# One load for Wq, held transposes, two QK bursts and twelve output buffers in a gated attention and token-MLP kernel

## Chip, cores and metric

The kernel runs on one core of one Trainium2 chip. The metric is device time in microseconds (us). Before: 175.59 us, the median of four executions. Most executions of this kernel lie within 0.3 us of their median.

The words used below: PE is the tensor engine, DVE the vector engine, ACT the scalar engine, SP the engine that issues the DMAs. A DMA lands when its semaphore reports it complete. An evacuation is the copy of a PE result out of its accumulator (`ps`) by DVE or ACT. bn_stats is the DVE instruction that collects the layer norm's mean and variance. A QK burst is a run of tiled matmuls that sums the logits, an AV burst one that sums the weighted values. The gelu bubble is the wait of PE for the last gelu (on ACT) between the two MLP products. A combine is the last line of the reference for one row tile. The granted clock is the share of PE's full clock that the trace shows; here it is 1 or a half. An execution counts as slow when it is over 1.5% above the fastest of the same kernel; slow ones are left out of the ratios, but not out of the medians.

## The reference, cut to what matters

```python
# x: (2048, 512) bf16; H = 32 heads of 16; window of 8 keys, dilation 2
g = sigmoid((x * gate_w).sum(-1))                  # one gate per row
a = attention(x @ wqkv) @ wo                       # 8 logits per query and head
b = transpose(gelu(layernorm(x)^T @ w1 + b1) @ w2 + b2)   # MLP over the 2048 rows, F = 1792
out = g * a + (1 - g) * b
```

On PE this is 48 groups of projections (four groups are split in two), two MLP matrix products of 224 matmuls each, 16 groups for wo, and small sums. The logits and the weighted values are products on DVE, which PE then sums with 0/1 matrices in tiled mode, several small matmuls side by side.

## The kernel before

A small scheduler written in Python orders the operations of every engine when the kernel is built; the order is static. The parts that the change touches:

```python
ld_x("sp", 0, 2); ld_x("sp", 2, 2)      # rows 0..511, 256 KB each
ld_w("sp", 0, 0, 2)                     # Wq, first half of the contraction, 256 KB
l_wq = ld_w("sp", 0, 2, 2)              # Wq, second half
l_wk = ld_w("sp", 1, 0, 4)              # Wk, 512 KB
ld_xt(1); ld_x("sp", 4, 4)              # DMA transposes of x and plain x blocks
ld_xt(2); ld_x("sp", 8, 4)
ld_xt(3); ld_x("sp", 12, 4)
ld_w("sp", 2, 0, 4)
# ... 7 warm-up matmuls, PE transposes of rows 0..511, evacuations on DVE and ACT ...
# first Q matmuls: halves of the contraction, so the first 16 need only the first half of Wq
for (dts, tps) in [((0, 1), (0,)), ((0, 1), (1,)), ((2, 3), (0, 1))]: ...
# ... QK: after every two DVE products (4.4 us each) one PE burst of 32 tiled matmuls; 4 bursts.
# The gate: 16 tiled matmuls on their own. ...
ds_out = [sch.dsem("out%d" % k) for k in range(4)]   # 4 output buffers, one semaphore each
for h in range(2): ...                  # the last tile goes out in two pieces of 256 columns
for d in ds_out: e.wait_ge(d.handle, 16 * n_)        # SP, at the very end
```

## Time and profile before

| read from | value |
|---|---|
| time, median of 4 | 175.59 us |
| span of the profile | 174.28 us |
| first Q matmul starts | 6.67 us |
| last output matmul starts | 171.09 us |
| last store lands | 173.81 us |

The first thing to settle is what bounds the kernel. The page of the kernel before says it in its busy shares (part 1) and in the chain that ended last (part 4):

```profile
PE 167.1 (96%) x1003; PEld 78.9 (45%) x1022; DVE 144.9 (83%) x146; ACT 74.3 (43%) x101; POOL 0.9 (0%) x8
...
PE 91%; DMA 3%; ACT 2%; issue 1%; SPq 1%; DVE 0%; DVEq 0%
```

DVE is 83% busy, but it takes none of the chain. The waits of PE, longest first, of the kernel before:

```profile
PE ps L610 <- DMA arena<-in_A_wqkv_dram: 1.5, 1, 1.5
PE ps L524 <- POOL arena L424: 1.1, 1, 1.1
PE ps L837 <- issue: 0.5, 3, 0.2
PE ps L876 <- ACT arena L850: 0.2, 1, 0.2
```

The columns are total us, number of waits, longest wait. Two waits at the front make 2.6 us of 3.3; L610 is the first Q matmul, and Wq is what it waits for. The timeline of PE at the front, kernel before (start, us, what, and in brackets the idle time ahead and what ended it):

```profile
1.06 3.07 PE L524 MATMUL ps<-arena 128*128 128x512 bf16 x7 [1.06 <-POOL arena L424]
3.96 1.17 PE L536 MATMUL ps<-arena 128*128 128x128 bf16 x16
6.67 3.66 PE L610 MATMUL ps<-arena 128*128 128x256 bf16 x32 [1.53 <-DMA arena<-in_A_wqkv_dram]
10.38 1.89 PE L587 MATMUL ps<-arena 128*128 128x512 bf16 x8
```

The four QK bursts are the lines of L688 in the PE timeline further on, x32 each, between ordinary matmuls:

```profile
43.05 1.91 PE L688 MATMUL ps<-arena 128*32 128x512 bf16 x32
44.89 7.10 PE L587 MATMUL ps<-arena 128*128 128x512 bf16 x31
51.91 1.91 PE L688 MATMUL ps<-arena 128*32 128x512 bf16 x32
53.98 6.85 PE L837 MATMUL ps<-arena 128*128 128x512 bf16 x31 [0.16 <-issue]
60.77 1.91 PE L688 MATMUL ps<-arena 128*32 128x512 bf16 x32
62.84 6.85 PE L837 MATMUL ps<-arena 128*128 128x512 bf16 x31 [0.16 <-issue]
69.62 1.91 PE L688 MATMUL ps<-arena 128*32 128x512 bf16 x32
```

No burst waits for its products: DVE does not set PE's pace here.

### The profile page before, as it was taken

What the parts mean: (1) busy time and instruction counts of PE and PEld (TensorE: products, weight loads), DVE (VectorE), ACT (ScalarE), POOL (GpSimd) and SP (SyncE); (2) the same over time, 40 slices, a digit from 0 to 9 for tenths busy, and PEclk for the clock granted to TensorE, in tenths of its full rate; (3) what the DMA queues carried; (4) which work ended last, traced back from release to release, by engine and by line L of the source; (5) the groups of instructions that cost most, each with busy time, mean ns of one, the idle gap of its engine ahead of it and who ended that gap; (6) DMA issues with size and microseconds to landing.
All of it is one profiled execution on the core that took longest, in us unless ns stands there. A gap on an engine that the chain in (4) does not pass through costs nothing.

```text
span 174.3 us, 2443 instructions
## 1 busy us (share of the span) xinstructions
PE 167.1 (96%) x1003; PEld 78.9 (45%) x1022; DVE 144.9 (83%) x146; ACT 74.3 (43%) x101; POOL 0.9 (0%) x8
## 2 busy tenths in 40 slices
PE   7699999999999999999999999999999999999993
PEld 3565554454444444444444443444444444444441
DVE  1707789799999999378999999999999999638824
ACT  2276668578367211679311315133521622270010
POOL 1000000000000000000000000000000000000000
PEclk9999999999999999999999999999999999999999
DMA  5999999920007079999999000073474370004413
GB/s 157 233 252 240 286 308 271 274 36 6 0 0 211 4 221 183 164 253 181 283 290 290 17 4 0 0 208 104 113 211 113 101 211 0 0 0 154 150 60 120
DMA packets 44862, 24.87 MB, mean 143 GB/s; under 512 B 7860, under 2 KB 44852, under 8 KB 44852
## 3 DMA queue, kind: packets, MB, share of 16 engines
q1 hardware_dynamic: 44852, 24.72, 58.9%
q8 instruction: 8, 0.13, 0.3%
q14 instruction: 2, 0.02, 0.0%
HBM read 18.88 MB, written 2.10 MB: 120 GB/s over the span
## 4 chain that ended last, share of the span: by engine, by line
PE 91%; DMA 3%; ACT 2%; issue 1%; SPq 1%; DVE 0%; DVEq 0%
PE ps L876 28%; PE ps L837 28%; PE ps L587 21%; PE ps L893 7%; PE ps L688 4%; DMA arena<-in_A_wqkv_dram 3%; PE ps L610 2%; PE ps L784 1%; ACT L653 1%; ACT arena L598 1%; PE ps L642 1%; SPq L437 1%; ACT arena L850 0%; DVE arena L917 0%; DVEq L331 0%
## 5 line engine op out<-in xcount | busy, mean ns | idle before, releaser
L876 PE MATMUL ps<-arena 128*128 128x512 bf16 x217 | 48.8, 379 | 0.6 <-ACT arena L850 0.2
L837 PE MATMUL ps<-arena 128*128 128x512 bf16 x218 | 48.0, 379 | 0.6 <-issue 0.5
L587 PE MATMUL ps<-arena 128*128 128x512 bf16 x171 | 38.5, 380 | 0.4
L776 DVE TENSOR_TENSOR arena<-arena 128x8192 bf16<-128x8192 bf16 x8 | 35.0, 4417 | 0.0
L681 DVE TENSOR_TENSOR arena<-arena 128x8192 bf16<-128x8192 bf16 x8 | 34.8, 4420 | 0.0
L876 PEld LDWEIGHTS ps<-arena 128*128 128x128 bf16 x224 | 21.5, 98 | 27.4 <-issue 1.2
L837 PEld LDWEIGHTS ps<-arena 128*128 128x128 bf16 x224 | 21.7, 98 | 27.0 <-issue 1.3
L940 ACT ACTIVATE arena<-ps,arena 128x512 bf16<-128x512 f32 x16 | 12.4, 776 | 37.5 <-PE ps L876 37.5
L587 PEld LDWEIGHTS ps<-arena 128*128 128x128 bf16 x176 | 19.5, 114 | 18.6 <-ACT arena L595 0.7
L598 ACT ACTIVATE arena<-ps 128x512 bf16<-128x512 f32 x32 | 18.9, 596 | 10.2 <-PE ps L587 10.1
L850 ACT ACTIVATE arena<-ps,arena 128x512 bf16<-128x512 f32 x14 | 9.6, 687 | 30.7 <-PE ps L837 30.6
L926 DVE SCALAR_TENSOR_TENSOR arena<-ps,arena 128x512 bf16<-128x512 f32 x15 | 11.2, 750 | 9.0 <-PE ps L893 7.5
L561 DVE BATCH_NORM_STATS2 arena<-arena 128x6 f32<-128x512 bf16 x16 | 10.1, 681 | 10.3 <-DMA arena<-in_A_x_dram 10.3
L893 PE MATMUL ps<-arena 128*128 128x512 bf16 x59 | 13.2, 379 | 0.1
L824 ACT ACTIVATE arena<-ps 128x512 bf16<-128x512 f32 (+1 forms) x7 | 8.0, 1146 | 4.3 <-PE ps L784 4.2
L803 DVE TENSOR_TENSOR arena<-arena 128x2048 bf16<-128x2048 bf16 x8 | 9.7, 1216 | 0.0
L806 DVE TENSOR_TENSOR arena<-arena 128x2048 bf16<-128x2048 bf16 x8 | 9.7, 1215 | 0.0
L729 DVE TENSOR_TENSOR arena<-arena 128x256 bf16<-128x256 bf16 (+4 forms) x16 | 7.8, 506 | 2.0 <-ACT arena L743 1.7
L810 DVE TENSOR_TENSOR arena<-arena 128x2048 bf16<-128x2048 bf16 x8 | 9.4, 1216 | 0.0
L893 PEld LDWEIGHTS ps<-arena 128*128 128x128 bf16 x60 | 5.9, 98 | 7.1
L595 ACT ACTIVATE arena<-ps 128x512 bf16<-128x512 f32 x12 | 7.1, 596 | 2.7 <-PE ps L587 2.7
L688 PE MATMUL ps<-arena 128*32 128x512 bf16 x128 | 7.6, 380 | 0.0
(56 smaller groups left out, 64.6 us busy)
## 6 DMA issues: line engine op xcount, KB each, us to landing
arena<-in_B_w_dram SPq DMA_DIRECT2D x7, 1024.0 KB, 9.7
arena<-in_B_w_dram SPq DMA_DIRECT2D x8, 896.0 KB, 5.1
arena<-arena SPq DMA_DIRECT2D x16, 131.5 KB, 5.9
out_dram<-arena SPq DMA_DIRECT2D x15, 128.0 KB, 1.7
arena<-in_A_x_dram SPq DMA_DIRECT2D x3, 512.0 KB, 4.6
arena<-in_A_wqkv_dram SPq DMA_DIRECT2D x2, 512.0 KB, 5.9
arena<-in_A_x_dram SPq DMA_DIRECT2D x2, 256.0 KB, 3.1
arena<-in_A_wqkv_dram SPq DMA_DIRECT2D x2, 256.0 KB, 4.8
```

Of the source, the lines that this page charges most:

```text
L561: A("dve", (lambda t_: (lambda e: e.bn_stats(out=ST6[:, t_, :], in_=X[:, t_, :])))(t), 0.7, reads=["x%d" % t], writes=["st6_%d" % t], name ...
L587: ins = e.matmul(ps[:, bank, :], lhsT=lhsT, rhs=XT[:, sb, dt, :], start=(dt == 0), stop=(dt == 3))
L598: return lambda e: e.activation(out=dst, in_=ps[:, bank, :], func=AF.Copy)
L681: return lambda e: e.tensor_tensor(out=PBL[buf], in0=in0, in1=in1, op=ALU.mult)
L688: ins = e.matmul(ps[32 * c:32 * c + 32, 4 + wl, :], lhsT=RP, rhs=PBL[buf][:, wl, c * 512:(c + 1) * 512], start=(dl == 0), stop=(dl == 3), ...
L776: return lambda e: e.tensor_tensor(out=PV[buf], in0=in0, in1=in1, op=ALU.mult)
L803: A("dve", (lambda b_: (lambda e: e.tensor_tensor(out=PV[b_][:, 0, :, :], in0=PV[b_][:, 0, :, :], in1=PV[b_][:, 1, :, :], op=ALU.add)))(bu ...
L837: ins = e.matmul(ps[:, bank, :], lhsT=W1W[:, slot, st, 128 * e_:128 * e_ + 128], rhs=X[:, st, :], start=(st == 0), stop=(st == NST - 1))
L876: ins = e.matmul(ps[:, bank, :], lhsT=W2S[slot][:, ft, 128 * e_:128 * e_ + 128], rhs=UT[:, ft, :], start=(ft == 0), stop=(ft == NFT - 1))
L893: ins = e.matmul(ps[:, WB(i), :], lhsT=OT[:, t, 128 * i:128 * i + 128], rhs=WO[:, t, :], start=(t == 0), stop=(t == 3))
L926: A("dve", (lambda i_: (lambda e: e.scalar_tensor_tensor(out=OUTS[:, i_ % 4, :], in0=ps[:, WB(i_), :], scalar=col(G, i_), in1=T1[:, i_, :] ...
L940: A("act", (lambda i_, bank_: (lambda e: e.activation(out=T1[:, i_, :], in_=ps[:, bank_, :], func=AF.Identity, scale=col(OMG, i_), bias=co ...
```

## The change

The intent: get Wq in sooner with one load that transposes do not disturb, free the front evacuations from bn_stats, pay for fewer switches into tiled mode, and never let an output buffer hold up a combine. Its core (cuts marked):

```diff
-        ld_w("sp", 0, 0, 2)
-        l_wq = ld_w("sp", 0, 2, 2)
-        l_wk = ld_w("sp", 1, 0, 4)
-        ld_xt(1)
-        ld_x("sp", 4, 4)
+        l_wq = ld_w("sp", 0, 0, 4)
+        ld_w("sp", 1, 0, 4)
+        ld_x("sp", 4, 4)
+        ld_xt(1, deps=[l_wq])
   ... (x blocks now ahead of the transposes; gate, bias and wo loads chained in order)
-        last_main[0] = front
-        for (dts, tps) in [((0, 1), (0,)), ((0, 1), (1,)), ((2, 3), (0, 1))]:
+        last_main[0] = A("pe", f_warm_on(NWARM2, 0), ...)          # NWARM2 = 3
+        for tp_ in range(2):
+            order0 = [(dt, tp_, dl) for dl in range(4) for dt in range(4)]
   ... (bn_stats of the first four tiles only after the evacuations on DVE)
   ... (the 16 normalisations get a low priority, to fill DVE while burst 1 runs)
+            def f_qk4(e, wh=wh):                                    # 64 matmuls, two bursts in all
+                r = [f_qkr(wh, dl, QKB[wh][dl])(e) for dl in range(4)]
+                return r + [f_gz(e)] if wh == 0 else r              # the gate behind the first
-        ds_out = [sch.dsem("out%d" % k) for k in range(4)]
+        ds_out = [sch.dsem("out%d" % k) for k in range(NOUT)]       # NOUT = 12
-            for h in range(2):
-                cs = slice(256 * h, 256 * h + 256)
+            for h, cs in enumerate((slice(0, 256), slice(256, 384), slice(384, 512))):
```

The products of a whole burst now need four buffers at once, so two more were laid over memory that is free at that time, and the output buffers were laid over the attention weights.

## The prediction

> **What bounds it now.** The tensor engine: the chain of waits is PE for 91%, and the PE timeline is continuous from 6.67 us (first Q matmul) to 171.36 (last output matmul), 164.7 of 174.3 us. The list of waits gives PE 3.3 us of idling, 2.6 of it before 6.67. DVE is 83% busy but costs PE no wait at the bursts. Only three places can pay: the front, extra cost inside the PE stream, and the tail (2.9 us).
>
> **Front: -0.75 us.** The first Q matmul waits 1.5 us for Wq (list of waits). The DMA issues show landings x 3.79 and 4.46, Wq halves 6.53 and 7.20, Wk 9.08. Undisturbed packets move 350 to 380 GB/s (0.7 us per 256 KB); from about 4.2 us, soon after the first transpose is issued (3.35), the same 1 KB packets take 66 to 71 ns instead of 47. With transposes held, 512 KB of Wq after 4.46 should land at about 5.9. Front evacuations ahead of bn_stats (680 ns each) are ready by then. The three extra warm-up matmuls end about 5.8. First Q matmul: 5.9.
>
> **Held transposes: +0.15 us (expectation).** The first starts at about 5.9 instead of 3.35, should land at 11.3 to 12.6, and is needed at 5.9 + 3.66 + 3.46 = 13.0. The last, now behind the last x block, should land at 20.6 to 22 (before: 20.88), needed at about 21.7: a stall of 0 to 1 us is possible.
>
> **Bursts: -0.55 us.** Tiled matmuls run 4 abreast, 57 ns each, so their own work stays. In the PE start times, entering a tiled group costs 308 ns against 216 between plain matmuls, leaving it 312: about 0.19 us per group. The Trainium skill ("TensorEngine Tiling (Array Packing)", Key Properties) says that changing the tiling mode drains the engine; the trace agrees, 0.19 us a round trip. Five groups (4 QK, 1 gate) become two: three round trips fewer. DVE cannot refill products while burst 1 runs (4.7 us), but 16 normalisations (0.33 us each) move into that gap. Attention should end about 1.5 us earlier, off PE's path.
>
> **AV bursts: +0.2 us (expectation).** The first AV burst (0.65 us at 106.1) now fills, by luck, the gelu bubble before the second MLP matmul. If it moves out, the bubble shows as a 0.9 us wait.
>
> **Tail: +0.3 us.** Twelve output buffers remove a 0.38 us DVE wait that PE did not feel. The last tile is stored in three pieces instead of two; an issue takes 0.46 us on the DMA queue, already back to back at the end (171.30, 171.69, 172.15), so one more delays the end by 0.3 to 0.45, less a slightly shorter last combine.
>
> **Sum.** 175.7 - 0.75 - 0.55 + 0.15 + 0.2 + 0.3 = 175.0; shaded to 174.8, since the order is made by a static scheduler that gets to fit the moved pieces. Range 173.8 to 176.2. Faster by over 2%: 2%; within 2%: 94%; slower by over 2%: 4%.
>
> **What would show it.** First Q matmul at 5.7 to 6.1, packets at 47 ns until then; no PE wait on x loads between 10 and 25 us; two QK groups of 64, 16 gate matmuls behind the first, no PE wait at either; PE stream first Q to last output matmul 164.1 to 164.5; gelu waits of PE under 0.9 us; tail 3.2 us.
>
> **What would make it wrong.** A burst placed before DVE has its products (PE stalls up to some us, since order is static); a late transpose or Wk; attention so late that DVE paces the last output matmuls.

## The result

The change takes 176.72 us against 175.59 before (medians of four), 1.13 us more. The ratio is 1.0064, with a 95% interval of 1.0047 to 1.0082. Ratios here and below are the mean time of one kernel's fast runs over that of the other's of the same rounds, so not quite the ratio of the medians. That is inside 2%, but outside the range that I gave (173.8 to 176.2), and on the other side of zero.

The page of the kernel after, the same two lines:

```profile
PE 167.9 (96%) x1011; PEld 80.8 (46%) x1029; DVE 145.8 (83%) x147; ACT 77.0 (44%) x103; POOL 0.9 (0%) x8
...
PE 76%; DVE 13%; ACT 6%; issue 3%; DVEq 0%; POOL 0%; POOLq 0%
```

DVE and ACT are in the chain now. That looks like a new bottleneck, but the waits of PE in the kernel after show what it costs:

```profile
PE ps L519 <- POOL arena L427: 1.1, 1, 1.1
PE ps L607 <- DVE arena L557: 0.6, 1, 0.6
PE ps L778 <- DVE arena L804: 0.2, 1, 0.2
PE ps L584 <- issue: 0.2, 1, 0.2
PE ps L831 <- issue: 0.2, 1, 0.2
```

The chain goes through DVE because the first AV burst (L778) waits 0.2 us for it. A chain shows where the last link was, not how tight it was. One releaser here is also a misreading: the first Q matmul (L607) is put down to bn_stats on DVE, an operation whose result it does not read. The landing times show that Wq came in at 6.89, 0.13 us ahead of that matmul, the same distance as before (6.53 to 6.67). The PE timeline of the front, kernel after:

```profile
1.06 3.17 PE L519 MATMUL ps<-arena 128*128 128x512 bf16 x7 [1.06 <-POOL arena L427]
4.02 1.80 PE L531 MATMUL ps<-arena 128*128 128x128 bf16 x16
5.66 0.81 PE L519 MATMUL ps<-arena 128*128 128x512 bf16 x3
7.02 3.66 PE L607 MATMUL ps<-arena 128*128 128x256 bf16 x32 [0.55 <-DVE arena L557]
```

The two bursts, PE timeline of the kernel after. No burst waits for its products here either; the burst matmuls are all there, in two groups:

```profile
44.87 3.64 PE L666 MATMUL ps<-arena 128*32 128x512 bf16 x64
48.33 1.04 PE L636 MATMUL ps<-arena 128*32 128x512 bf16 x16
49.54 4.26 PE L584 MATMUL ps<-arena 128*128 128x512 bf16 x19 [0.17 <-issue]
53.64 15.70 PE L831 MATMUL ps<-arena 128*128 128x512 bf16 x71
69.27 3.64 PE L666 MATMUL ps<-arena 128*32 128x512 bf16 x64
```

A kernel that is one unbroken PE stream can be cut at four milestones, and the pieces add up to the span. These times are from the records of the two traces:

| piece | before, us | after, us | difference | predicted |
|---|---|---|---|---|
| start to first Q matmul | 6.67 | 7.02 | +0.36 | -0.75 |
| first Q to last output matmul (starts) | 164.42 | 163.78 | -0.64 | -0.20 |
| last output matmul (start) to last landing | 2.73 | 3.13 | +0.40 | +0.30 |
| last landing to end of span | 0.47 | 1.04 | +0.57 | 0 |
| span | 174.28 | 174.97 | +0.69 | |

(The -0.20 is -0.55 for the bursts with the two expectations of +0.15 and +0.2.) The middle came out better than I said; the front and the last row came out worse. The table explains 0.69 of 1.13 us. The rest is the front of this one execution of before: the run that was profiled took 176.0 us, 0.4 above the median, and a second profile of the same kernel (run b_same below) had its first Q matmul at 6.12 and a span of 173.79, 1.18 below the kernel after. The granted clock was 0.998 to 1.0 in all four timed executions of the kernel after, so the half clock that comes up below is no part of the 1.13 us.

### The profile page after: what moved, and what is told of

Its sections match the earlier page's. It is cut to its first block, busy times and chain, and to the rows that moved or that the text cites. A ratio compares the mean times of both kernels' runs of the same rounds, so it can differ in the third digit from the quotient of the medians.

```text
span 175.0 us, 2471 instructions
## 1 busy us (share of the span) xinstructions
PE 167.9 (96%) x1011; PEld 80.8 (46%) x1029; DVE 145.8 (83%) x147; ACT 77.0 (44%) x103; POOL 0.9 (0%) x8
## 4 chain that ended last, share of the span: by engine, by line
PE 76%; DVE 13%; ACT 6%; issue 3%; DVEq 0%; POOL 0%; POOLq 0%
PE ps L870 28%; PE ps L584 20%; PE ps L831 9%; PE ps L887 7%; DVE arena L770 5%; PE ps L666 4%; ACT arena L737 2%; PE ps L607 2%; PE ps L519 2%; PE ps L778 1%; DVE arena L723 1%; DVE arena L804 1%; DVE arena L797 1%; DVE arena L800 1%; DVE arena L748 1%
## 5 line engine op out<-in xcount | busy, mean ns | idle before, releaser
L708 ACT ACTIVATE arena<-ps 128x1024 bf16<-128x1024 f32 x4 | 4.0, 1021 | 8.5 <-PE ps L666 4.6
```

## The experiments

All kernels gave correct results. In the first four and in the kernel after, the traces show the same order of PE's groups, of DVE and of ACT apart from the named edit. From f_oldfront on, the order of every engine behind the front is frozen to that of the changed kernel, by giving the scheduler a list, because it otherwise moves bursts and output matmuls at the far end when a load at the front changes. Times are medians of five or six executions.

### 1. The changed kernel with Wq in two loads: a_split

```diff
-        l_wq = ld_w("sp", 0, 0, 4)
+        ld_w("sp", 0, 0, 2)
+        l_wq = ld_w("sp", 0, 2, 2)
   (and the order of the first Q matmuls by halves, as before)
```

> The changed kernel with Wq in two 256 KB loads again and the first Q matmuls in the order of before (first half of the contraction first); the transposes stay held, all else as changed. Theory A (one 512 KB load makes PE wait for the last byte of all of Wq, and without the transposes the first half could land at 5.3 to 5.9 us): first Q matmul at 5.9 to 6.4 us instead of 7.02, then limited by the extra warm-up, and the time falls 0.6 to 1.1 us, to about 175.8. Rival B (Wq itself moves slowly whatever its cut; the cut is innocent): first half lands at 6.5 or later, first Q at 6.7 or later, time within 0.3 us of the changed kernel.

Measured: 176.42 us, ratio to before 1.0039 (1.0017 to 1.0060). The first half landed at 6.03, but the first Q matmul started at 6.88. The clock of PE was at half until 6.74 us in that execution, and the three extra warm-up matmuls, which run ahead of it in program order, started at 5.72, ran mostly at that half clock and held it up. The ratio is 0.0025 below that of the changed kernel (about 0.4 us), with overlapping intervals. Neither theory was cleanly met: the half came early, as A said, and something else held PE.

### 2. The changed kernel without the hold: a_nohold

```diff
-        ld_xt(1, deps=[l_wq])
+        ld_xt(1)
```

> The changed kernel with the first transpose no longer held for Wq: only its wait on Wq is taken out, so it is issued right behind the x block, at about 3.4 us. If transposes in flight slow Wq, as I predicted: Wq lands later than 6.89, at 7.2 to 7.6, and the time rises 0.3 to 0.7 us. If the hold is useless: Wq lands at 6.9 within 0.15 us and the time is the same within 0.15 us, with the transposed x blocks landing 1 to 3 us earlier.

Measured: 176.84 us, ratio 1.0080 (1.0055 to 1.0104). Wq landed at 6.46 in the profile, 0.43 earlier than with the hold in the profile of the kernel after. The time does not separate the two kernels: the intervals of their ratios overlap. So with the x block in between, no gain from the hold is seen, and the packets that I had put down to transposes are slow without them too: in the trace of the kernel after, where the first transpose is issued at 6.90, the rate falls to 242 GB/s around 4.0 us and to 213 to 279 GB/s from 5.25 to 6.5 us. Single packets of 1 KB take up to 1.0 us between 3.5 and 7 us there, and up to 0.4 us in a_nohold. All kept profiles together say the same: from 4.0 to 6.5 us the DMA engines moved 256 GB/s on average in the eight profiles with a hold and 250 in the ten without, and both groups range from about 205 to 300.

### 3. The end: a_waits and a_nout4

```diff
-                for d in ds_out:
+                for d in sorted(ds_out, key=<start of its last store>):     # a_waits
-NOUT = 12
+NOUT = 4                                                                  # a_nout4
```

> The changed kernel with the same twelve output buffers and twelve semaphores, but the waits at the very end taken in the order in which the stores are issued, so that the wait for the last store comes last. Theory C (waits that come behind the one for the last landing cost time at the end: the trace shows the last landing at 173.93 and the end at 175.0, against 173.81 and 174.3 before): the stretch from last landing to end falls from 1.07 to 0.5 us and the time falls by 0.4 to 0.6 us. Rival (the end is longer because there are more semaphores, not because of the order): no change beyond 0.1 us.

> The changed kernel with four output buffers and four semaphores, all engines' orders the same. Theory C: the stretch from last landing to end is 0.45 to 0.6 us as before, time falls 0.4 to 0.6 us; the DVE wait on a store comes back (about 0.4 us) without effect on the end. If twelve buffers were worth something: the time rises or falls less than 0.2 us.

Measured: a_waits 177.13 us, ratio 1.0089 (1.0062 to 1.0115); a_nout4 176.72 us, ratio 1.0059 (1.0031 to 1.0088). The times scatter by over 1 us here (the front again: first Q matmul at 7.34 and 7.72), but the last piece of the span does not: from last landing to end it is 0.90 us in a_waits and 0.47 us in a_nout4, against 1.03 to 1.06 in all profiles with twelve buffers and the waits as changed. So the order of the waits is worth 0.14 us of the 0.57, and theory C gave it too much; four buffers give all of it back. The end of SP in the records of the kernel after (start, us, what it waits for):

```text
172.38  DMA, last piece of the last tile; lands at 173.93
173.06  wait, 0.897 us: the semaphore of the last store
174.02  wait, already satisfied
174.10  wait, already satisfied
174.58  branch to the end        <- 0.45 us after the wait before it had ended
```

In the kernel before, the branch comes 0.05 us after its last wait.

### 4. Yardsticks: a_same and b_same

> The changed kernel itself once more, as the yardstick for this chip and for the scatter of its front: four profiles of kernels with the undivided Wq load had it land at 6.46 to 7.58 us. Expected: time 1.0 to 1.5 us above before, first Q matmul 6.7 to 7.7 us, 163.8 us from there to the start of the last output matmul, 1.04 us from the last landing to the end.

> The kernel before itself, for a second profile of it. Expected: first half of Wq lands at 6.0 to 6.6, first Q matmul at 6.2 to 6.8 us, 164.4 us from there to the start of the last output matmul, 0.47 us from last landing to end; time ratio 1.000 within 0.002.

Measured: a_same 177.45 us, ratio 1.0087 (1.0067 to 1.0107), with executions from 176.65 to 179.42; the median is 1.8 us above before, more than the 1.0 to 1.5 expected. b_same 175.69 us, ratio 1.0004 (0.9992 to 1.0017), from 175.52 to 175.86. The kernel before is tight; the changed kernel is not. The profile of a_same fell on its slowest execution, and it is not used for any difference, but it shows one source of the scatter: Wq landed at 7.92, PE waited 1.9 us for it, and then the granted clock was at half from 8.26 to 11.67 us. b_same differs from my expectation only in that its first Q matmul came a little earlier than I had put it, 6.12.

### 5. Old front, old end: f_oldfront and f_best

```diff
 f_oldfront
   (loads, first Q matmuls, warm-up and bn_stats at the front as before)
         total_est = sch.schedule()
+        sch.freeze(FROZEN)        # engine orders of the changed kernel behind the front
 f_best, on top of it
-NOUT = 12
+NOUT = 4
-            for h, cs in enumerate((slice(0, 256), slice(256, 384), slice(384, 512))):
+            for h, cs in enumerate((slice(0, 256), slice(256, 512))):
```

f_oldfront is the changed kernel with the whole old front. f_best is f_oldfront with NOUT = 4 and the last tile in two pieces, so that of the change only the bursts, what belongs to them and the order of the loads behind the front are left.

> The changed kernel with the whole front of before put back (two Wq loads, first transpose not held and ahead of the x block, no extra warm-up, bn_stats mixed with the evacuations, Q matmuls by halves); every engine's order behind the front is frozen to that of the changed kernel. Theory F (the new front costs time: PE waits for the last byte of 512 KB instead of 256, or for the extra warm-up at half clock): first Q matmul 6.2 to 6.8 us, time 0.4 to 0.9 us below the changed kernel on this chip. Rival (the new front is neutral, the loss is all at the end): time within 0.2 us of the changed kernel.

> As f_oldfront, with four output buffers and the last tile in two pieces, so that of the change only the bursts, the moved normalisations and the order of loads behind the front are left. If my account is right (stream -0.65, front 0, tail as before): time 0.4 to 0.7 us below before, and about 0.9 us below f_oldfront, with 0.47 us from last landing to end. If the end of the changed kernel is slow for another reason, it stays within 0.2 us of f_oldfront.

Measured: f_oldfront 176.13 us, ratio 1.0032 (1.0017 to 1.0046), 1.3 us below the changed kernel on the same chip (a_same; 1.0 us by the ratios). One of its six executions was slow, 178.89 us with a mean granted clock of 0.986. f_best 175.12 us, ratio 0.9972 (0.9960 to 0.9984). First Q matmuls at 6.16 and 6.34. f_best is 0.5 us below before and 1.0 below f_oldfront, as expected. So the new front costs 1.0 to 1.3 us there (more than the 0.9 that I gave as the most), the new end costs 1.0 us, and what is left of the change is a gain: f_best beats both kernels. Its stretch from first Q to last output matmul is 163.73 us, 0.69 and 0.75 less than in the two profiles of before.

From the last output matmul to the last landing, all seven profiles with three pieces that were taken up to here show 3.12 to 3.13 us; f_best, with two, shows 2.80, and so do the later kernels with two. The third piece costs 0.33 us.

### 6. Single parts put into f_best: g_oneload, g_hold, g_warm, g_waits8

```diff
 g_oneload
-        ld_w("sp", 0, 0, 2)
-        l_wq = ld_w("sp", 0, 2, 2)
+        l_wq = ld_w("sp", 0, 0, 4)
 g_hold
-        ld_xt(1)
         ld_x("sp", 4, 4)
+        ld_xt(1, deps=[l_wq])          # x blocks ahead of transposes 2 and 3 too
 g_warm
+        last_main[0] = A("pe", f_warm_on(3, 0), ...)   # ahead of the first Q matmul
 g_waits8
+                for d in sch.dsems[:8]:                # long satisfied
+                    e.wait_ge(d.handle, 16)
                 for d in ds_out: ...
```

> The best kernel so far (f_best, 175.12 us, 0.5 below before) with one thing of the new front put in: Wq in one 512 KB load. Theory G (the undivided load is what costs: the first Q matmul waits for the last byte of all of it, 0.7 to 1.9 us behind the first half in the profiles, and a long wait lets the clock drop to half for 3.4 us in some executions): first Q matmul at 6.7 to 8 us instead of 6.1 to 6.4, time 0.5 to 1.3 us above f_best with a wide scatter (some executions 1.5 us or more above the lowest). Rival (the load is innocent, the warm-up or the hold costs): within 0.2 us of 175.1 and as tight.

> f_best with only the new order of the other front loads put in: x block ahead of the first transpose, transpose held until all of Wq is in. If my prediction was right that transposes in flight slow Wq: the first half lands at 5.3 to 5.8 and the time falls by 0.4 us or more. If the slow packets come without transposes too, as the profiles of the held kernels show: first half at 6.0 to 6.6 as in f_best, time within 0.2 us of 175.1.

> f_best with only the three extra warm-up matmuls put in ahead of the first Q matmul. If the clock is already full when they start (5.1 us) they end at 5.8 and cost nothing; if it is still half (three profiles show it turning full only at 6.3 to 6.7) they run at 0.43 us each from 5.7 and hold the first Q matmul until about 6.9. Expected: time 0 to 0.4 us above 175.1, 0.2 on average. If they keep the clock from dropping instead, time below 175.1 by 0.1 or more.

> f_best, four output buffers, with eight more waits put ahead of the four at the very end, on semaphores that were satisfied long before, so that the queue engine has twelve waits there as in the changed kernel, but none of the eight for a store. If the number of waits (length of the program at the end) makes the 0.57 us: about 0.43 us of it comes back from last landing to end (0.9 instead of 0.47) although no wait comes behind the last landing that wasn't there. If it is the twelve stores' own semaphores: 0.47 us and 175.1 as f_best.

Measured:

| run | time, us | ratio to before | first Q, us | last landing to end |
|---|---|---|---|---|
| g_oneload | 178.41 (176.76 to 179.72) | 1.0133 (1.0097 to 1.0170) | 8.79 | 0.48 |
| g_hold | 174.77 | 0.9971 (0.9936 to 1.0006) | 5.99 | 0.47 |
| g_warm | 174.93 | 0.9965 (0.9948 to 0.9981) | 6.18 | 0.47 |
| g_waits8 | 175.49 | 0.9993 (0.9977 to 1.0009) | 6.49 | 0.89 |

Of the parts of the new front put in alone here, only the undivided load costs time. It costs 3.3 us over f_best (2.8 by the ratios; the chips differ), which is more than the whole new front did. Not put in alone was the move of bn_stats behind the evacuations. The profile of g_oneload has two faces of it. One is the wait of PE:

```profile
PE ps L641 <- DMA arena<-in_A_wqkv_dram: 3.4, 1, 3.4
```

The other is the clock. The table of stretches for g_oneload (stretch and its length, busy time and count of PE, PEld, DVE, ACT, POOL, then the granted TensorE clock, DMA share, GB/s), and under it the same stretches of f_best:

```profile
5.20:8.10 2.90, 0.20 (x4) 0.03 (x1) 2.37 (x8) 0.88 (x2) 0.00 (x0) 1.00 1.20 291
8.10:11.50 3.40, 2.71 (x13) 1.97 (x14) 0.00 (x0) 0.00 (x0) 0.00 (x0) 0.50 1.02 163
11.50:14.90 3.40, 3.35 (x27) 2.76 (x26) 0.70 (x2) 2.30 (x5) 0.00 (x0) 1.00 1.06 264
```

```profile
5.20:8.10 2.90, 2.49 (x24) 2.25 (x23) 2.49 (x8) 1.11 (x2) 0.00 (x0) 1.00 1.11 316
8.10:11.50 3.40, 3.40 (x26) 2.65 (x24) 0.00 (x0) 2.67 (x5) 0.00 (x0) 1.00 1.03 250
11.50:14.90 3.40, 3.40 (x18) 1.80 (x16) 2.23 (x4) 2.34 (x4) 0.00 (x0) 1.00 1.10 235
```

While PE idles, the clock stays full; the stretch after that is granted half. In it the first Q matmuls of g_oneload start every 213 ns, those of f_best every 109. From first Q to last output matmul g_oneload takes 165.04 us instead of 163.73, so the half clock costs 1.3 us on top of the wait. It is not all of the scatter: the slowest execution of g_oneload, 179.72 us, had a mean granted clock of 1.0, as had the fastest. The Trainium skill ("TensorE: Matmul & The Clock Gate", Part 1: The HAM clock gate) says that half rate is what PE falls back to after an idle window of about 3.4 us, and that the windows run free of the program. The trace agrees in length: the half-clock record is 3,413 ns long, and so is the full-clock record ahead of it (4.69 to 8.11). That window was not quite idle: PE ran transposes for 0.71 us of it.

g_hold lands the first half at 5.85, in a band between the two theories (5.3 to 5.8, and 6.0 to 6.6). The first halves with a hold landed at 5.85 and 6.03 so far and without one at 5.99 to 6.53. A gain of 0.2 us from the hold is possible, and the time (174.77 against 175.12 in another job) does not contradict it, but the interval includes no change against before, mainly because of one execution at 176.68. g_warm shows no cost of the extra warm-up, against my expectation of 0 to 0.4; in its profile the clock was full at 4.94. g_waits8 brings 0.42 us of the 0.57 back at the end, with the same 0.45 us pause between the last wait and the branch, though none of its eight extra waits comes behind the last landing. So what costs there is the length of SP's program, not the stores. (The time, 175.49 against 175.12, says the same.) The kept traces sharpen this: in all seven profiles with twelve waits the pause (0.44 to 0.47 us) follows the 79th instruction that the trace records of SP, whatever comes next. In a_split and f_oldfront, which have one load more, that is a wait and not the branch. A program with four waits has at most 78 records, and no such pause behind its last wait. Why the pause arises at this place, the trace does not show.

### 7. What the undivided load costs by what: h_waitboth, h_onebusy, h_onehold, h_combo

h_waitboth is f_best with two loads but the changed order of the first Q matmuls, so that the third needs both halves. h_onebusy is g_oneload with eight warm-up matmuls ahead of the first Q matmul. h_onehold is g_oneload with the hold. h_combo is f_best with the hold and three warm-up matmuls.

> f_best (two Wq loads) with only the order of the first Q matmuls of the changed kernel, so that the third matmul needs both halves. In eight profiles of two loads the second half landed at 6.58 to 7.85, mean 7.1. If waiting for all of Wq is the cost: third Q matmul at about 7.2, time 0.5 to 1.1 us above f_best's 175.1. If one 512 KB load is itself slower than two: much less than g_oneload's 3.3 us here, at most 1.1, and the rest belongs to the load being one.

> g_oneload (one Wq load, 178.4 us) with eight extra warm-up matmuls ahead of the first Q matmul, which keep PE busy until 7 to 8 us. In its profile g_oneload lost 1.3 us behind the first Q matmul because the clock was at half from 8.11 to 11.52. If the clock falls because PE idles while it waits for Wq: no half clock after the front, 163.7 us from first Q to last output matmul instead of 165.0, time 177.0 to 177.4. If the clock falls for another reason: it falls here too and the time stays at 178.4.

> g_oneload with the transposes held until Wq is in and the x block ahead of them, as in the change. The changed kernel and its variants with one load had it at 6.46 to 7.92, against 8.66 in g_oneload where the transpose was issued at 2.88. If transposes in flight slow the undivided load: Wq lands at 6.5 to 7.9, time 176.0 to 177.0, 1.4 us or more below g_oneload. If 8.66 was chance: no difference beyond scatter, 178.

> f_best with what did not hurt of the new front: transposes held (g_hold 174.77) and three warm-up matmuls (g_warm 174.93), Wq in two loads. If both are small gains that add: 174.5 to 174.7, ratio to before about 0.994. If they are noise or the warm-up holds the earlier Wq back: 174.8 to 175.2.

Measured:

| run | time, us | ratio to before | Wq all in, us | half clock in |
|---|---|---|---|---|
| h_waitboth | 176.00 (175.56 to 178.26) | 1.0033 (0.9993 to 1.0072) | 7.63 | 2 of 6 executions |
| h_onebusy | 176.39 (175.57 to 176.98) | 1.0034 (1.0010 to 1.0058) | 7.19 | 0 of 6 |
| h_onehold | 177.18 (175.61 to 178.77) | 1.0068 (1.0031 to 1.0105) | 7.88 | 2 of 6 |
| h_combo | 175.14 | 0.9967 (0.9952 to 0.9983) | 7.05 | 0 of 6 |

The last column counts executions whose mean granted clock is 0.99 instead of 0.996 or more; g_oneload has four of six. The half clock is not peculiar to the undivided load: f_oldfront and, in the rounds of g_oneload, the kernel before each have one slow execution whose mean clock (0.986 and 0.99) points to it. h_waitboth costs 0.9 us over f_best and over h_combo, which ran on its chip, although its loads are exactly those of f_best. The PE timeline of its front shows the third Q matmul waiting:

```profile
6.18 0.38 PE L642 MATMUL ps<-arena 128*128 128x256 bf16 x2 [0.27 <-DVE arena L593]
7.67 3.46 PE L642 MATMUL ps<-arena 128*128 128x256 bf16 x30 [1.11 <-DMA arena<-in_A_wqkv_dram]
```

In f_best, the same lines are one unbroken run:

```profile
6.34 3.66 PE L642 MATMUL ps<-arena 128*128 128x256 bf16 x32 [0.41 <-DMA arena<-in_A_wqkv_dram]
```

So the wait for all of Wq instead of its first half costs nearly what the whole new front costs (1.0 to 1.3 us). It is not most of the 3.3 us of g_oneload. The rest there goes with the load being one: it came in late (8.66 in the profile), and four executions had the half clock. h_onebusy has the loads of g_oneload and no half clock behind the front in any execution, with the stretch from first Q to last output matmul back at 163.73 us; the expected time of 177.0 to 177.4 was too high, because Wq came in at 7.19 this time. With six executions, and h_onehold at two of six on the same chip, this supports an idle PE as what loses the clock, but does not settle it. The same stretches of h_onebusy, to hold against the two fences above:

```profile
5.20:8.10 2.90, 2.90 (x20) 1.91 (x19) 2.49 (x8) 1.11 (x2) 0.00 (x0) 1.00 1.10 294
8.10:11.50 3.40, 3.40 (x32) 3.19 (x31) 0.00 (x0) 1.54 (x4) 0.00 (x0) 1.00 1.04 197
```

h_onehold is 1.2 us below g_oneload, but on another chip and with a scatter of 3 us, so what the hold does for an undivided load stays open. h_combo is f_best within 0.1 us: nothing of the new front pays beyond the scatter. Also open: why one load of 512 KB came in as late as 8.66 us in g_oneload, 1.5 us behind the mean of the second halves of two loads and behind h_onebusy, which has the same loads (7.19).

## Why the prediction was wrong

**Front: the step that failed.** The prediction said: "With transposes held, 512 KB of Wq after 4.46 should land at about 5.9", and so first Q at 5.9. It took the rate at which the sixteen DMA engines move bytes together (0.7 us per 256 KB) for the time at which one load is complete. In the kernel after, 1,024 KB (x and Wq) were needed. As many bytes had been moved in all by 5.73 us, so the rate itself was not wrong; but Wq was reported in only at 6.89, when about 1,350 KB had been moved. In g_oneload it was about 1,610 KB at 8.66. The surplus had gone to later loads. The Trainium skill ("DMA: Bandwidth & Descriptors", section "Why a DMA increments its semaphore by 16 and not by 1") says that a DMA runs on up to 16 engines that finish independently and that only the full count means that all data has landed. The traces agree: in the eight profiles with one load, 167 to 586 KB beyond the needed 1,024 had been moved when it was reported in. For the second halves of two loads it was 221 to 569 KB, so cutting the load does not cure this; it only lets PE start earlier. Which engine is late the trace does not tell. In ten profiles with two loads, the first half landed at 5.85 to 6.53 us (mean 6.1) and the second at 6.58 to 7.85 (mean 7.2); in eight with one load, all of it landed at 6.46 to 8.66 (mean 7.5). Two loads let PE start on 256 KB, and the 16 matmuls of the first half (1.8 us) cover the wait for the second. The change gave this cover up. Added to it, in some executions, is a cost that the prediction did not have at all: PE lost its full clock after the wait, which cost 1.3 us in the profile of g_oneload. It is not in the 1.13 us.

**The cause that I named for the slow packets was not shown, at most a small part.** Transposes were issued at 3.35 and packets were slow from about 4.2, so I put one down to the other. The slow stretch comes in every profile, held or not, and is as deep on average in both (256 and 250 GB/s). One coincidence in one trace was not enough.

**Held transposes: right.** No PE wait on x between 10 and 25 us; the transposes landed at 11.82, 16.16 and 21.56, in the ranges given for the first and the last, before they were needed. The expected 0.15 us was 0.

**Bursts: right, and a little too small.** Predicted -0.55 us for three fewer round trips of 0.19 us; measured -0.69 and -0.75 (f_best against the two profiles of before). The round trip was a little under-counted: the first gap inside a group is 217 ns instead of 206, and the first one behind it 226 to 244 instead of 216, which makes it 0.21 to 0.23 us, three of them 0.63 to 0.68.

**Attention "about 1.5 us earlier": wrong, without effect.** The last DVE product came 0.4 us earlier, but then the second burst carried 64 matmuls and not 32, and DVE waits for it. The DVE timeline of before and of after where the softmax goes on:

```profile
72.66 0.12 DVE L723 MEMSET arena<- 32x8 bf16 x4 [2.67 <-ACT arena L714]
```

```profile
74.04 0.12 DVE L717 MEMSET arena<- 32x8 bf16 x4 [4.41 <-ACT arena L708]
```

Attention is 1.4 us later. PE has other work in that time, and only the first AV burst notices, with 0.2 us. It still fell into the gelu bubble: the 0.2 us wait of PE on gelu (L876) in the kernel before is gone, and this one stands in its place, so the +0.2 us of the prediction was 0.

**Tail: one term right, one missing.** The third piece was put at 0.3 to 0.45 less a shorter combine; it costs 0.33. The 0.57 us at the end, from the eight more waits in SP's program and from their order, was not in the sum.

**The sum.** With the measured terms: bursts -0.7, third piece with its combine +0.4, waits at the end +0.57, front +0.9 (7.02 against 6.12 in the second profile of before), together +1.2 us, against 1.13 measured. The predicted 0.15 and 0.2 fall away.

## What to carry to other kernels

A consumer that starts on part of a load should get that part as a load of its own: a load is reported in only when the last of its engines is done, and some of the bytes moved by then (167 to 586 KB here) belong to what is queued behind. Count the instructions behind the last transfer as carefully as those ahead of the first, since waits and semaphores at the very end are on the critical path whatever bounds the middle. And when a change has several parts, freeze the order of everything else and put the parts in one at a time; here a gain of 0.5 us was hidden under losses of over 1.5 us.

## What the Trainium skill lacked or had wrong

- "TensorE: Matmul & The Clock Gate" speaks of an idle window of about 3.4 us. The window need not be empty: in a_same PE was busy for 1.48 of the 3.42 us ahead of the half clock, of which three ordinary matmuls took 0.81 and the first Q matmuls 0.2; the rest were transposes, as were all of the 0.71 us in g_oneload. In h_onehold a window with 1.52 of 3.41 us busy was not followed by half clock. Where the border lies, these runs do not say.
- The same page puts the first transition at about 4 us into matmul activity, with 500 ns of variation. With the same warm-up from 1.06 us on, the clock turned full at 3.9 to 6.7 us in these profiles, 2.8 to 5.7 us into the activity. (From 4.0 us on that activity is transposes, so it is not the back-to-back matmuls that the page speaks of.)
- No page has a figure for waits at the end of a program. Eight more waits, satisfied long before, made the end 0.42 us later (g_waits8); with twelve waits there is a pause of 0.44 to 0.47 us behind the 79th recorded instruction of SP that is not there with four.
- "DMA: Bandwidth & Descriptors" says that the engines of a DMA finish independently, but not by how much: here a load of 512 KB was reported in when 167 to 586 KB beyond what was needed had already been moved.
